# Logits copied ahead of the lower half of v, and a new order table, in a bucketed-attention and mixture-of-experts kernel

## The chip, the cores and the metric

The kernel runs on one core of a Trainium2 chip. Its time is the device time of one execution in microseconds (us); before the change it is 607.02 us, the median of three runs (606.85 to 607.43). The engines are TensorE (PE in the profile, its weight loads PEld), VectorE (DVE), ScalarE (ACT), GpSimd (POOL) and SyncE (SP), on whose queue nearly all DMAs are issued. Each engine takes its instructions in the order in which they were issued to it.

## The reference

Two layers follow each other, over 4 batches of 768 positions.

```python
# attention: 8 heads of 64; q and k are hashed to 6 sign bits each
q_bits = (q @ proj) > 0 ;  k_bits = (k @ proj) > 0        # 6 bits -> bucket
scores = where(q_bucket == k_bucket, (q @ k.T) / 8, -1e9)
x = softmax(scores) @ v                                   # heads side by side: 512 columns
# mixture of 4 experts, each a causal attention of width 64
logits = x @ w_gate                                       # 4 per position
topk = two largest logits;  w = softmax over these two
for e in range(4):
    qe, ke, ve = x @ wq[e], x @ wk[e], x @ wv[e]
    ye = softmax(causal(qe @ ke.T / 8)) @ ve @ wo[e]
    out += (e in topk) * w_e * ye
```

Everything is float32 in the reference. The kernel computes its products from pairs of float16 numbers, a high half and a low half.

## The kernel before, in words

**The units of work.** There are 32 units "L" (batch, head) of the first layer and 16 units "M" (batch, expert) of the second. `s_unit` (line 946) does one unit in chunks of up to 512 columns: two products into a PSUM tile `st`, two exponentials on ScalarE (`p` in float32, `ph` in float16), their difference `pl` on GpSimd, and three products per 128 columns into the PSUM tile `o`, with `ph` and `pl` against the high and low halves of v. `max_steps` (line 799) finds each row's largest score two units ahead: products into a PSUM tile `mx`, and VectorE's reductions of it into `pm`. A chunk of the lists `L_MAX`, `M_MAX` and `M_S` (lines 787 to 795) may have two parts; for these two products go into different columns of one tile, and each part is reduced by an instruction of its own. `shift_steps` (line 871) turns the maxima into a row: a product into `misc`, a copy to `row` on ScalarE or VectorE, and a DMA into the unit's `qa`, which the unit's `st` products read. `normalise` (line 1044) divides `o` by its sums; of the last unit it does a first half while products of the other half are still to come.

**The jobs beside them.** `prep_pair` and `proj_steps` make q and k, `xt_steps` transposes the first layer's result, `vproj_steps` (line 1118) makes v of the four experts and the gate's logits, `gate_steps` the gate's weights, `out_steps` and `last_out_steps` the output. `vproj_steps` has six tiles of 128 positions per batch, 24 in all: twelve products of 260 columns into a `misc` tile, then three readers of that tile: ScalarE writes the high half of v (`mvh`), VectorE the low half (`mvl`), and ScalarE or VectorE copies the 4 logits columns (`lg`).

**PSUM tiles.** Eight banks: three `st`, two `mx`, two `misc`, one `o`. Two engines' accesses to one tile are put in sequence in the order in which they are issued, whether or not they touch the same columns, readers among themselves too.

**The order.** The functions don't issue anything. They record 11,117 operations in a list (`Recorder.add`), some with two engines to choose from (`Recorder.copy`, line 128, offers ScalarE first and VectorE second). `Recorder.schedule` (line 163) then reads the table `ORDER` (line 216): compressed, four bytes for each operation. Two bytes say which of the operations still left is issued next, one which of its engines it takes, and one how many filler products (128 by 128 of ones, into the `o` tile) are issued ahead of it. So the table alone decides each engine's sequence, SP's and POOL's too, and the recorded list only gives the numbers that the table's places refer to.

```python
for take, alt, fill in zip((raw[0] + 256 * raw[1]).tolist(), raw[2].tolist(), raw[3].tolist()):
    order += [self.filler] * fill
    o = left.pop(take)
    order.append((o, o.alts[alt]))
```

All operations are issued by line 185, which is why every row of the profile has that line; rows are told apart by the tiles that they write and read.

Of the kernel before, what the change touches and what calls it, by code (L numbers as in the profile page):

```python
# [18 lines left out]
AX = mybir.AxisListType  # L19
# [96 lines left out]
class Recorder:  # L116
# [173 lines left out]
def tile_kernel(ctx, tc, q, k, v, proj, w_gate, wq, wk, wv, wo, out):  # L290
    nc = Recorder(tc.nc)
    B, HP, _, _, HS = q.shape
    _, KT, E, D = wq.shape
    Dm = KT * 128
    H, S = 2 * HP, 2 * HS
# [70 lines left out]
    for g in range(4):  # L366
        o = 32 * g
# [21 lines left out]
    for j in range(2):  # L389
        x = pbe[D * j:D * j + D, j]  # L390
# [143 lines left out]
    U = {}  # L534
# [538 lines left out]
    XT, G, XS = {}, {}, {}  # L1073
# [394 lines left out]
```

## Time and profile before

| | before |
|---|---|
| median of three runs | 607.02 us |
| the profiled execution's own time | 607.13 us |
| its span, first to last instruction | 605.3 us |
| TensorE busy, matmuls | 590.1 us |
| VectorE busy | 523.7 us |
| ScalarE busy | 516.7 us |
| GpSimd busy | 471.4 us |
| DMA, mean over the span | 85 GB/s |

The span is one profiled execution. A busy time counts an engine's instructions, not its waits; matmuls overlap one another and their ends are modelled, so that TensorE's busy time is no measure of how full the array is. A time in brackets behind a row is how long the engine sat idle before it, and the name behind the arrow is what ended that idle time.

### The profile page before, as it was taken

What the parts mean: (1) busy time and instruction counts of PE and PEld (TensorE: products, weight loads), DVE (VectorE), ACT (ScalarE), POOL (GpSimd) and SP (SyncE); (2) the same over time, 40 slices, a digit from 0 to 9 for tenths busy, and PEclk for the clock granted to TensorE, in tenths of its full rate; (3) what the DMA queues carried; (4) which work ended last, traced back from release to release, by engine and by line L of the source; (5) the groups of instructions that cost most, each with busy time, mean ns of one, the idle gap of its engine ahead of it and who ended that gap; (6) DMA issues with size and microseconds to landing.
All of it is one profiled execution on the core that took longest, in us unless ns stands there. A gap on an engine that the chain in (4) does not pass through costs nothing.

```text
span 605.3 us, 20342 instructions
## 1 busy us (share of the span) xinstructions
PE 590.1 (97%) x7754; PEld 432.6 (71%) x7754; DVE 523.7 (87%) x1440; ACT 516.7 (85%) x1132; POOL 471.4 (78%) x540
## 2 busy tenths in 40 slices
PE   7999999999999999999999999999999999999996
PEld 4788888778776777777667676777767677767663
DVE  6999999898899999888979999988988977557973
ACT  7989999999889899968969999997978978935774
POOL 8899989977687999858777889985866888942661
PEclk9999999999999999999999999999999999999999
DMA  6666353231512132341323143222222121001322
GB/s 189 170 191 191 86 139 78 53 101 52 147 46 57 40 91 61 85 122 26 98 81 95 38 117 102 60 86 76 69 88 82 46 48 36 17 21 35 89 72 106
DMA packets 36314, 51.23 MB, mean 85 GB/s; under 512 B 8212, under 2 KB 26104, under 8 KB 36216
## 3 DMA queue, kind: packets, MB, share of 16 engines
q1 hardware_dynamic: 36056, 49.93, 30.0%
q8 instruction: 61, 1.00, 0.7%
q14 instruction: 37, 0.30, 0.2%
q10 hardware_dynamic: 160, 0.00, 0.0%
HBM read 20.98 MB, written 6.29 MB: 45 GB/s over the span
## 4 chain that ended last, share of the span: by engine, by line
PE 78%; ACT 8%; DVE 8%; POOL 2%; issue 2%; DMA 2%; SPq 0%; DVEq 0%; ACTq 0%; POOLq 0%
PE misc L185 24%; PE st L185 24%; PE o L185 19%; PE mx L185 12%; ACT p L185 3%; ACT ph L185 2%; DVE pm L185 2%; POOL pl L185 1%; DVE pmw L185 1%; ACT xt L185 1%; DVE xt L185 1%; DMA qk<-M 1%; DVE qk L185 1%; DMA pbe<-in_proj_dram 0%; DVE scrap L185 0%
## 5 line engine op out<-in xcount | busy, mean ns | idle before, releaser
L185 POOL TENSOR_TENSOR pl<-p,ph 128x512 f16<-128x512 f32 x370 | 409.5, 1127 | 106.4 <-ACT p L185 31.2
L185 PE MATMUL st<-qk,qk 128*128 128x512 f16 (+12 forms) x928 | 229.8, 325 | 2.3 <-ACT p L185 1.2
L185 ACT ACTIVATE ph<-st 128x512 f16<-128x512 f32 x372 | 213.7, 609 | 13.3 <-PE st L185 9.2
L185 ACT ACTIVATE p<-st 128x512 f32<-128x512 f32 x372 | 215.5, 608 | 11.2 <-PE st L185 8.1
L185 PEld LDWEIGHTS <-ph 128*128 128x128 f16 x2880 | 168.2, 98 | 35.2 <-issue 5.8
L185 DVE TENSOR_REDUCE pm<-mx 128x2 f32<-128x512 f32 (+1 forms) x248 | 163.1, 674 | 10.6 <-PE mx L185 7.7
L185 PEld LDWEIGHTS <-pl 128*128 128x128 f16 x1440 | 133.3, 97 | 16.8 <-issue 4.2
L185 PEld LDWEIGHTS <-qk 128*128 128x128 f16 (+4 forms) x1248 | 109.1, 98 | 43.2 <-issue 6.8
L185 PE MATMUL o<-vh,ph 128*128 128x65 f16 (+1 forms) x1104 | 138.8, 194 | 0.3 <-DVE xp L185 0.3
L185 PE MATMUL o<-vh,pl 128*128 128x65 f16 (+1 forms) x1104 | 138.8, 193 | 0.3 <-POOL pl L185 0.3
L185 PE MATMUL o<-vl,ph 128*128 128x64 f16 x1104 | 138.2, 192 | 0.0
L185 PE MATMUL mx<-qk,qk 76*128 76x512 f16 (+2 forms) x464 | 134.3, 326 | 2.8 <-DVE pm L185 2.5
L185 PE MATMUL misc<-xt,wqk_h 128*128 128x384 f16 x256 | 58.6, 325 | 0.1
L185 DVE CUSTOM_DVE_ANT_0 scrap<-mx,causal 128x512 bf16<-128x512 f32 (+2 forms) x96 | 44.5, 463 | 8.0 <-PE mx L185 6.2
L185 DVE TENSOR_REDUCE pmw<-mx 128x2 f32<-128x512 f32 x68 | 44.9, 682 | 2.3 <-PE mx L185 2.0
L185 PE MATMUL o<-mvh,pl 128*128 128x65 f16 x336 | 40.6, 193 | 0.6 <-DVE yn L185 0.6
L185 PE MATMUL o<-mvl,ph 128*128 128x64 f16 x336 | 40.9, 192 | 0.0
L185 PE MATMUL o<-mvh,ph 128*128 128x65 f16 x336 | 40.6, 194 | 0.1
L185 POOL TENSOR_TENSOR vl<-vf,vh 128x384 f16<-128x384 f32 x32 | 29.5, 925 | 10.6 <-PE misc L185 5.1
L185 PEld LDWEIGHTS <-xt 128*128 128x128 f16 x324 | 29.5, 97 | 10.4 <-issue 1.2
L185 PEld LDWEIGHTS <-wqk_h 128*128 128x128 f16 x256 | 24.1, 97 | 13.9 <-issue 0.8
L185 PE MATMUL misc<-wvg_h,xt 128*128 128x260 f16 x192 | 32.1, 274 | 0.7 <-ACT row L185 0.7
(226 smaller groups left out, 1001.6 us busy)
## 6 DMA issues: line engine op xcount, KB each, us to landing
qk<-qk SPq DMA_DIRECT2D x128, 96.0 KB
natv<-in_v_dram SPq DMA_DIRECT2D x16, 384.0 KB
natq<-in_q_dram SPq DMA_DIRECT2D x15, 384.0 KB
natk<-in_k_dram SPq DMA_DIRECT2D x15, 384.0 KB
out_dram<-ot SPq DMA_DIRECT2D x20, 256.0 KB
qk<-qk SPq DMA_DIRECT2D x96, 48.0 KB
qk<-qk SPq DMA_DIRECT2D x8, 192.0 KB
qk<-M SPq DMA_DIRECT2D x48, 24.0 KB
```

The costliest lines, as they stand in the source:

```text
L185: getattr(getattr(self.nc, e), m)(*[real(x) for x in args], **{k: real(x) for k, x in kw.items()})
```

## The change

It has two parts. In `vproj_steps` the copy of the logits is recorded ahead of the low half of v:

```diff
             nc.scalar.activation(MVH[:, i, :, 0:D], pv, AF.Copy, scale=2.0 ** -16)
+            nc.copy(lg[:, i], p[:, E * D:W], XS[b][:, 2:3])
             nc.vector.scalar_tensor_tensor(MVL[:, i], pv, 2.0 ** -16, MVH[:, i, :, 0:D], op0=OP.mult, op1=OP.subtract)
-            nc.copy(lg[:, i], p[:, E * D:W], XS[b][:, 2:3])
             yield 864
```

And the table is another one; of its text only the beginning is shown:

```diff
 ORDER = (
-    "c-rlJX^bT2d0u^A-S^#9)z#Hqec#9QOwUZubkEGr%+9gPy}3M>BE4K*wnBljgy^6sSdb`LzLX$jC_r)|IdG6fN}@!8%mju5<X;5A2y6sF{v<G9|L_k(K%D%E6XpG?yLV=m%ZL=0<nFQ`"
...
+    "c-rlpX^b3adf)4<`|i5Bx~i+Y`o8a(>1%qrd+r&|3`vn39y*qi)+9wrkyc#El6E&<%ZTh`y^yiHh-Jg;>^d?wae%$xtdm{Ci2)-H5CaAh_=ADKK`tZ+VC;t=UMC2QAkSMpJu{>ztqw}0"
...
```

Decoded, both tables hold the same 11,117 operations, 7,609 of them products on TensorE. What differs:

- The sequence on every engine; the median product on TensorE stands 3 places from where it stood.
- Products into a PSUM tile and readers of that tile. In both tables 71 products stand behind a reader of the same tile (40 in `shift_steps`, 16 in `prep_v`, 15 into `o`). In the old table 19 more do: 11 into `mx`, 4 into `o` behind the first half of the last `normalise`, 1 into `st` behind the addition of the causal mask to the tile's other part, and 3 of the constants at the start. In the new table these 19 stand ahead of all readers of their tile.
- The readers of the 24 tiles of `vproj_steps`. The old table has 8 with `lg`, `mvh`, `mvl` in that sequence, 5 with `mvh`, `lg`, `mvl` and 11 with `mvh`, `mvl`, `lg`. The new table has `mvh`, `lg`, `mvl` in all.
- The engine of 85 operations: ScalarE has 1,152 instead of 1,149 of all operations, VectorE 1,341 instead of 1,344, GpSimd 536 as before. `lg` is copied by ScalarE 19 times instead of 13.
- The fillers, 87 instead of 75, all among the first 72 products; 26 instead of 8 stand ahead of the first product of the sign rows (`mx<-natq,pbe`).

## Rows read from the trace of the kernel before

**Rows 1.** The page: busy us of each engine, share of the span, instructions.

```profile
PE 590.1 (97%) x7754; PEld 432.6 (71%) x7754; DVE 523.7 (87%) x1440; ACT 516.7 (85%) x1132; POOL 471.4 (78%) x540
```

**Rows 2.** The page: the chain that ended last, share of the span by engine.

```profile
PE 78%; ACT 8%; DVE 8%; POOL 2%; issue 2%; DMA 2%; SPq 0%; DVEq 0%; ACTq 0%; POOLq 0%
```

**Rows 3.** Stretches: from:to, us, busy PE, PEld, DVE, ACT, POOL (instructions), PEclk, DMA share, GB/s.

```profile
180.00:210.00 30.00, 28.98 (x403) 20.60 (x400) 28.34 (x76) 28.23 (x62) 25.49 (x25) 1.00 0.20 49
...
360.00:390.00 30.00, 29.80 (x452) 21.90 (x450) 28.36 (x77) 29.02 (x65) 26.30 (x27) 1.00 0.35 95
```

**Rows 4.** Timeline at seven places of TensorE: start us, us, engine, line, operation [idle before <-releaser].

```profile
156.57 0.19 PE L185 MATMUL o<-vl,ph 128*128 128x64 f16 x1
156.86 0.55 DVE L185 TENSOR_REDUCE pm<-mx 128x1 f32<-128x384 f32 x1
157.46 0.22 PE L185 MATMUL mx<-qk,qk 65*128 65x128 f16 x1 [0.69 <-DVE pm L185]
...
180.09 0.34 PE L185 MATMUL o<-vs,fq 128*128 128x65 f16 x6
...
194.68 0.19 PE L185 MATMUL o<-vl,ph 128*128 128x64 f16 x1
195.64 0.22 PE L185 MATMUL mx<-qk,qk 65*128 65x128 f16 x1 [0.77 <-DVE pm L185]
...
370.95 0.19 PE L185 MATMUL o<-vh,ph 128*128 128x66 f16 x1
371.34 0.22 PE L185 MATMUL mx<-qk,qk 65*128 65x128 f16 x1 [0.20 <-DVE pm L185]
...
481.10 0.32 PE L185 MATMUL misc<-xt,wqk_l 128*128 128x384 f16 x1
481.87 0.22 PE L185 MATMUL mx<-qk,qk 65*128 65x128 f16 x1 [0.45 <-DVE pm L185]
...
544.15 0.19 PE L185 MATMUL o<-mvh,ph 128*128 128x65 f16 x1
544.50 0.27 PE L185 MATMUL mx<-qk,qk 65*128 65x256 f16 x1 [0.16 <-DVE pm L185]
...
586.44 0.38 PE L185 MATMUL st<-qk,qk 128*128 128x384 f16 x2
587.28 0.33 PE L185 MATMUL st<-qk,qk 128*128 128x128 f16 x2 [0.46 <-DVE st L185]
...
592.64 0.38 PE L185 MATMUL mx<-wo_h,xt 128*128 128x512 f16 x1
593.64 0.19 PE L185 MATMUL o<-mvh,pl 128*128 128x65 f16 x1 [0.62 <-DVE yn L185]
```

**Rows 5.** The logits' tile: copies on ACT (ns min/median/max); what ended idle time before (us, times).

```profile
L185 ACT ACTIVATE lg<-misc,xs x13: 239/263/265, 148.5 to 552.7; 128x4 f32<-128x4 f32 x13
...
  DVE mvl L185: 3.6, 6
```

**Rows 6.** Shift rows: a DMA in the chain, then the timeline of two units.

```profile
368.11 1.74 DMA qk<-row
...
179.93 0.27 ACT L185 ACTIVATE row<-misc 12x128 f16<-12x128 f32 x1 [0.61 <-DVE fr L185]
182.54 0.38 PE L185 MATMUL st<-qk,qk 78*128 78x512 f16 x1
...
461.96 0.25 ACT L185 ACTIVATE row<-misc 12x128 f16<-12x128 f32 x1
464.92 0.68 SPq L185 DMA_DIRECT2D qk<-row  x1
```

**Rows 7.** Timeline of the first 17 us.

```profile
3.66 1.49 PE L185 MATMUL mx<-natq,pbe 128*32 128x384 f32 x2
...
6.57 0.81 PE L185 MATMUL mx<-natq,pbe 128*32 128x384 f32 x2
...
14.32 1.80 ACT L185 ACTIVATE xt<-xt 64x384 fp32r<-64x384 f32 x3
```

More of the change, by code (lines that the diff above doesn't have):

```diff
@@ new lines @@
+    "mrf)TNw49Qh*GJ@6beEqUn=Gcc0T84eLwB{zN<QgLfp;eyl0>N+3bssldRrw-4aupa|(uh*(0K9;F0vztNBN+pL^=zaG3dvOemeUABme6A5s0s9=qiGmoHn%)P?9vvDk|*irTBM4uAjW"
+    "4cBp2&?a|dPq23!C;S;FWRHoJu({g)lKS`TvZ=iGTD4d~8Le{%G&a)>sjXJ)#1vKC0+u#6H`P-cEl~lA#kn>7tQd{<1oy^`8(~-PURB1*KMz@rW$ROi%(0I?nn=j5F&|4CX7bwG@X|{!"
+    "+4hS8@(WWcmHlwocl3y!xvuNZ^768-k4B@-&H0^&Eqz_z+;1A)#;DO4?d@s1ySwVnjuG@)8w?jKX9fe?uIc)4IIOg9$_q<NdZXJJ4$FqI2o(BtnZjc}LN-bzM=2D{Xx&Xzt5v(zQXMDa"
+    "gfGgLRZF{=;4ybdI7?*KZ8McJlgV&6pEo0x9Qul`n@0Z2c^y8EZ*1h4Y&l<=Ams|T(LRnVr=m_1NHmTSPu85vx**1j@vQ6lK5p1=l)Si~%BAATjFyhY`u)*J`xP(#Wf<<z_xnC37LUiP"
@@ new lines @@
+    "a%_U+P3Qxz2a{!4H`HV@DJBw$6NySC;#;g4HiJ<nCj6O1kVC_;@~ira4%45}v~)OZ7^bOt#sM1}ne6=OjFugb$9jsd)oN?~z7fsm^DO&NY{2dBKite_v+al|+P|Ij53ZajegFH(;y9P^"
+    "#cY6-Nja%osoh4ZTK&1~XGu7?+fAl(o|xg{4Y$=gbqYr5yK!%8tGxGEvE)YAw)AJ8&EtWbN~QP0yH13EYRjGwnTtd?`!=*NCVfOWra5z_-H63Zk2c)@=ZeNZV=6kM<3-G5*4O{$L}5L%"
+    "xtdp*>?r>>;7*&rnf#M{KAkS4;f-|m&J+q+&r4@A>8i@?Crf^!P)KdU4ERwuHeOo?(&<E;_Pu8oJ+J4{!Ftl3_o?Tr_3E?F!lG6#mBlZ7!8u1e0iW7?K1I{vBrOWlbvkN|zLGgYHzmXH"
+    "jfC#UbS)bNFQ9Xai=j|DgqI-HYSlTOtI*9VOojA}cZ>szE-^9j_JNO%fHe>Vr+0vpNEC}v$IZpEg8|G=wt7gc=2!mIEv-%XSI+8$=%RB%7`gfnI+5SiSKBKK%dz(QIx|}N7DP9;Ic0dj"
@@ new lines @@
+    "SH8lS;n!>J1rf)yU&IfOV$4U5s6ULMQFY6bu8hZ)HX8nDtc8?NK6J#A)e470p}_ErxgKFaBlUXs5Vbn-SaD%OZ5{|oySOtIRVzp9TmeSaDV5^xT(MB;M-z!?a0Z#ryVdwg;Mq%Cyca93"
+    "dFA7rnG&l<;&IO>Yum{!H&*tdnNz12$9GB5_3SK7+OZ^UvT?>R!aX=|VR`|lRx0fthuN^K;c$Bt4r^B5(#)}G47DW&79<kc59sXeojKF#pWZnYa+qBe*xEeKg#djuIG8yHoS>+OFq(8~"
+    "Jcbn;@2^6p__ied&M6t@ufH?crVg!O>xkiaj177{28%md87-^hu??YRd1Zb1#M&CQ##xcYMQUONJiih^YDPFrk|qvaPaLv)eoi}a_Uzf6t0y>pN(d}?dwV;Kn>uBm9h^}@2PSoLWLkqU"
+    "V;ZsbBTQp;wccGEcl&|)^p_49o3yg8o$EoWh^+Nj^^X4Ja=YK(SbB8f)2o`^xqMkW9~mwL$NumPepJ%0w%fhqJUnVGcF}x)*#BE<E?L{lW_Rv{c7jT$L!bYAQ7pe~C4LqNQ8@qk{>__l"
@@ new lines @@
+    "W%0S^p8MuEP46EZ;wi>&n6CG06Wll6xbnsuYw;<LllH)M1wlfH3Www2m<z$$bsv+3@D-i3tQ1m<#jdI%o0K8fD@s;QL3~LilGW<xs#Tdm*sXIp)M~A)z}jEC=3QlzG?`8&9)G-i86Xo&"
+    "Y@yI8fJvb90eF=b=3===A06$DnvXxe^vf5UOU?aXWL|r1<4j}y5_|64!7?z|t1oqGwezZaPKD(=`!i>cSXp}Lq4H_qvqvneqtft|i{WQ3JpJ^}jT<|~@YeR3#nTMKocioH0qz@XB>DBP"
+    "fBpLP>%We9;mtRLiFx4-V0r82&98m!%{QrkNd4AZxboSr(iHU@G~NF)K9=qeuU$pd&fe<)&oA&i|M~S-DDHo9-126N+y27(2KV{Tzy1ox{qob#zxbu&h$1HlMULke;UxY#&vUN;q9|W@"
+    "@xtZHH*elVtXo_7r!2>n*(s^r?*z{~so&mbiE|9g_Rhe|z1`hkQLkSQKlRj8;cF*$AgqMpT?1k@`}1t-Bo51xR4lgJCsS-P3G>cwY%D*5jadyqAkCsK7HD!~?wGpKw&73I^&}=Ym(1pL"
@@ new lines @@
+    "J<X76v{>@X4kg=4I1D<c(}~M+BGKa|>3j89Y;KNkRk{&~RiapGR!fajmC7W?IH?<x=aJ(K3DXgTu;;}+uhTIi5D*<}&Jv%udewTJFik>lUeXbt;Teugpaj9}=65nVcyT*pj+<sIqf%CR"
+    "QpRJFQwqpBJf;}@x!(i4_F}v3Eo}Z{wkKhrNvSDG%^p0|>vc&|D*wA6k)k}o7c-!S2I6|+bDnq$3pZ|*%c@eYa6+*NUL%Miw$q3kSzb=~5g{f7*lBn$jOWH<c-D2Te6{z-qF5Jfl?l|a"
+    "lE^BG6!YX;v85m5D}G&?u7aW<<yLI_i(d@>K?@Qu%Df~<^6rzSX>Ln2FYuQxfzx!iP-i0$DPehJ9fvm?3?u9_Vj}2Akc{m4d2()Ujs@>-S*1pUt{<?6aVJS3!NeH|l4!HI5ib@C%RPIP"
+    "9FK>i(U5L;LZBWk2$#oc^oK{B1ct-lLZKjtnNhl-I<*B=YiJttWK~&&K=CS8+NbctBHe7#B}Pglo~8X_achfC)6CDTtv&f9mj<!ur*LNG1{gj?9oa*=%*pE<Hu$2XP#%@ZMAJ$tr36--"
@@ new lines @@
+    "R9*Zi$W$yy)M+>>?ClmJScF95={TQ?C%}QKi3GhE6S#Pklm1Q=(2}(4hOWLutL3tNN!KkeCq$#BscV96Artgz$cV>Db)s}^BnO5LUMS`ueQFRcrHsB?+)3!kZ~x&RhQy5{z@c#HU-=6z"
+    "COiM=xGBKmtB@H3gI42lH40C^l$1e|Mm)xb158=wDq=_!!Pk^(^%<}yco!AGx-;~ly@Do;xr>XU=<;Bd^A1a{>1Lnfz!nf<WC)Atv?wRjaB8-km1RbV#l&=)=D6^ReKfI(%qj4ss+<C5"
+    "RxHAmA#!DL_~Icp9mFV_!O#-~us(WijbnG9o~9u)(BRGz&b>4Wk}q{E+Hn7lP!A{_;S`zqKeFT0arL{p$}rI|Pt)-@6{O8rJ=AV9V8_(_Jk_0}z5$dL7MjgP=|?SzDpYATTQQ2?{jOZd"
+    "SLzf+tyb;~wz~?;LQ(P>=g}<dB#1-3nadqUVnh(AW04go=mp_XS>b$56!qv?l9eJ6@n`{)x3I9l<3fh@eK!7UobHo(uq(Izy7o6U=4+8ksBD)?zF)8-aXacWM$Gqr9Q)gGCIm`Gwm~8l"
@@ new lines @@
+    "uNOgJCqp`v8!&gQ%Knv`^E@}ox>@&pMvmAM>pN=SI7Xph7%Z#Np;MtylH5t9GQ)ofD>B^JP}kS}AN*h~rmn0E`+aXk4PwiJ6+9tXCTfIuAaWHoC&iOW97iuj5#?89aV0ECsMq8EtDx$F"
+    "h6CR;Oy#dAl)&Y3d@8q*!}>xXMx(?q&a#PJc4tR-JMM@jTqo3I4uQqbLG)IX9JByUz*`ZAN!Ws52}evuL~+`IhlHdci@}0TZ61;<q)twx_7p*Yl7a?z0E1)^6&eoVb6o0Cuvil)dSMbO"
+    "FNC>$Dh-{WSdO7^Q$GBGLiW6DHg80;bjqDpn-KeGQv(^t4gQC~_4~?Tz|j{kPOiw>r%%^$q1e3@qEu>z!&?l?QE=7u>{^Loc!)iGwc4&$^I(Dt6&@n79B&qjH~>S!r5QH{h2Y|17Cy*k"
+    "Q}Y2XooY5GJ*iaaa+#un3Vvd%X)jFEE`5mTk<qB&PQU}Druz{buka4f6$*6xFuSn-;lIljHmD4w63_p8?XU2aheNPCt{)0@yCa_B7_TTXq7tbVi^}6-cQSuT5A0kge68YWmr%&%ovh<n"
@@ new lines @@
+    "md(ItxCF(~`j-ZS-X6u7n89FvzTaP6m70IOEJ-gt^UR1H)~Tlk13?gb!jT~hpg78xgp!lo7YI8ZPx7~5n$V-Epzm}h&k7hv;UTVAd`OO+;yh^=N~7&4nv^GN8yliH2u!6jwHezcBndjT"
+    "P;Qu}4CBgxktJ~@Z0zic>pGbC23&K9Rgw80MFURk$g-;4PFc=?`JF$XOqz)}s3HLul_65FtTkI`%r(HGCYjhU3&AXK8g#cf>Gc(!w|Ety5F{N&Ai!+po+wFejh1Dw@5vJJ0{BISPs7lY"
+    "w@n4l69mgjEUUAcMv0WlhG>dz4QRg6qxf$3(j|(5z&wSHP`Bx+TXt0blv8ysC=wLQOj0syOtwGfZiN+_VXMYwD;2Q43P(|?bgGtPg-rF0W-(JPR3~DhP^r@SQlVJP-?pVS(fAXXT#hV("
+    "UMQ6Y^?IgIW%3M@P3AM@a<Vw@q?{&mxNC6ofK-NMSN%ho?65Yycz|3eK!V%V^|?&1)xr}z$MdAB{u|YExb90Oe&vtqI4Dm?0_OU=oDhW3B1qVEx)6;nf3;G{9aPHSEtlgUeuiMpxv<A_"
@@ new lines @@
+    "?KUe$q3909L@!#7svhk)prM;h^JMs}ey|T^!>kw-4>=Q1I)zXiR2Z2uj6l5%6uqopighk@f?XQM^G=?WLXuP_OR^k~29^@IsvIOg67M=q7LO15NvdFNppt?GgM?&yy2mHU1ns!H4|5!$"
+    "v%O_KP`uHo3L=K6-~dGy{sm+&lQURaV?+7rP6nsq$m(#HAWPXYBpDzi$zKFm35zQ3<(FSBKzs#-CGpQC@Qx7g`-$g|TMe4pWQ^w#>p14nV%eV@t`7_C@Ijt$@hrz<*PAZ|9>`9Hg*bfF"
+    "A5RYEIEKS!udz~le6`JSOG^y5!Z1AnjD%&b)v65JWlk~;Y`lLT{+Ry+XIc2v>`{|<$o0*NtJNc{;;PN&kS;aAzwk!h=s4@}m(G_*in6YRm_AK+heMDV6Gcle-2yQf(2GnT%8veazt!w0"
+    ";D%kc(_!0zCDvJ<>%i!^iJ=w5=}y$tichivWJNZ;EeNF&%i`wu_xGoc%7yWSDvHV3df9@{)DZTZ9!Ei-_?=M5Yl0Qm;7?*~2aFSh!6X%Um00;!y#FkSg~H+fil5)u5U#UpYq6LAjE^#!"
@@ new lines @@
+    "X2u5tA9`#$mL0RjQmGXdEijpkuA50Ckp-!v|69Cm!b16D+bVpN&tsdi;&#%u6}P7>|HvPAz-~P+ZyDeF-a+!C^>$k{=b4a66bdzLXd!UO)K{~iq?U=Nv+QQ#u*RWex!>2du_bqVJz0KE"
+    "o@~~%)YI5ZcXwYGb}AJ~Vsa(4l)kk-6R}`lj+&w)>jnsL9AdL6vyl?vm6%dvdC%L9#}gYHUeXVR1O|&{g9%(j;^%J<=O8d7iuaIo0K!eEV5}hUd76VNd<Eppw^%gV+7ek7G9Ax{4}i=o"
+    "=(lkoC;4Nh*qS_j`qQkdM96p!va31z7Go~W(;&cUwcX~y>Z*|S%}6VNZvG}PSCW|qRj(_*_j?tZ25pzjedjyh5i?x<Hn`N&DgIZpRDu3#G@8sLlf`1PQaRA2(3$LESE3UeNuuKQIgpz!"
+    "&oEfkKL!bhr1c2Bk7d1#bE{TFzfa|V_(KTy5_TMxTa%x&uu`xDhUfeJ{-sO2?r4$QK=e=Om6a7l;caA`OcY6HY8rM5QDg#T*Jxxz7oaRDV`)d{;^?*-IXVHku7C|Q0tqq1hj<8n1@V-;"
@@ new lines @@
+    "c=Du-gH=4b`3HZnxw+I?5(WcToYbUFR9yNe5y5sA7CJ(hv%WEjRBGvs$v+O<E#cuReq}{~BJQuJnN{xwPtQ%ulxtj`gUNfM%Kd9maI-jcCArvPCM69Rl40ZU1Fld~K~aDu!Yid%WZ`rP"
+    ";=GUIQU6PUT|rSJm=VKqVDWLe6<kB$g3n6bE-$j#?4)zm8jDl%@ucrfo>)#C?~HG<`e(LSc4MQ(3Z^Ltx@k%+<BqUgnq;_${lD<OyjZvsc<=TclV%Js6*KBj?5~A)Vrsab)vCR|eyMnL"
+    "ONx<L#7o(9tCeY`@dfbVl`f0-VlU<E_48bg6LvD0CV&274L+v1(;&z^4{u0qjyNWEP~{~Tk}*goOfm@;c2prS8FYdY<#-(19N3ZEcX~4KN=F=xZk|vnD#&XvT@uA`1idHFJ3Bnj!1M;$"
+    "g&hfJV2XtOKZgpGg9?FVn>)_iFkmAL(`9g|&{{z|OqQmD`uzKGkAFi#9M^(aZ5}O59)d-Z7oe{_p;k*Q#0CG_HNRN&{mW2V{M>)J9LHXF(IX1{q?(@GO*)N|$3>ZS2Wrh4uEH4EP#7ie"
@@ new lines @@
+    "CQqJ>#df!LcD9l}4x?+rs?1EM1o|$_&5Lu`-LMb?#8#=Q7G<!=Jk(Pp5eF5)bCHO5IFFq2BOK`frO}kYK&o}{Jt<!*Nw?#-#RznBgVQ3Gy&NJ(C5yt1Xa>UsL6iwG8C)3VA=VP%R4N*U"
+    "=qRih%hQ-0q3Q5~#_}o)4}6z{Yz)_Bp*jkP$6;#I4z%GPPKq4nI78%Uo^6lE!UDH+`LZ;?6)vsTrY@@Tu16!vrvBT3W8*T?At<}8Q!MM=MoN~aQR)_bYuL>uWGrgXq#HDiw<WTf2F*}e"
+    "5aE>y7<r>mPZz4UlCRJ?d?;Nkt{0(ttW?U!w!_Nhdbvhdt86+w$E2FsO16A>X028|ckY$I?U>-cPO<oZBaxHGU}G!`g4biu9q1dXRKjD+Q|tWvFI*rY&79Rieuk=50cv)7lcm6_n$7VT"
+    "1jkadDY-7gKq!h9tVSd6{uZN7TFz>j%pB9w@+k(&&8%vgSkD#1VJIkZ0oMzM@jWT^%tik1X2QB{c({B(fv{C4;etiOpsdte3L}~gO;^=UCmIdG^m06C@x-A4rz|JI`gqI3&*v>7%UkVs"
@@ L287 @@
+    "eBuJi%<X4!bH<Dr@5!Ojy%JvNUNm~2tpNIfmqd4YQqbKTF}e$_&2rLAS<E_lzfBaHEyqVS5_G?Ia`tn`SzP`I%oNSc?GvBG(0wx(=o7mJ_p=G0nZv&K>mu}lyM#VD>yI8}3qudU^q`;e"
+    "4*G<x`V8Xk|92Dj+&9q7EN7;B7p{ih#V7BfJ2Qj)2=v-)j^5qud=ROK-sv#(p)Umb_?hJg>^}O?f8FtsPU}aWpWkV;=mB%=kE_F>kKeSSd(i0pw8M)YESEs{!|dD-zY;++W4ebUMDMk@"
+    "_=xTHeK+^ML)Tr1dGGoX=x$3DDR>OM%cF1qY5tvmm1q(ge!BC|n%?<`+#l#?j`-x+kNjuMm@#9<j2Sa#%$PA_#*7&=X3Ur|W5$dbGiJ<~F=NJz88c?gm@#9<j2Sa#+?oFm&mr{="
 )
```

86 lines of the change are left out of this document (17 added, 69 removed).

## The prediction

> **What bounds the kernel now.** I read four views, from the coarse to the fine. The page's table of engines comes first: TensorE is busy 97% of the span, VectorE 87%, ScalarE 85%, GpSimd 78% [rows 1]. The reader is to see that no second engine is at its limit over the whole span, and that TensorE leaves 605.3 - 590.1 = 15.2 us idle. The chain that ended last says the same: 78% of it is PE, and ACT and DVE have 8% each [rows 2]. So only two things shorten this kernel: less TensorE work, of which the change removes none, or fewer waits of TensorE. The table by stretches then tells where another engine could take over: DVE is at 28.3 and ACT at 28.2 of 30 us between 180 and 210, ACT at 29.0 between 360 and 390 [rows 3]; over the whole span they have 4 us idle in 30. Last comes the timeline of PE alone, where a wait is a late start with its releaser in brackets.
>
> **The waits that the change is about.** TensorE takes its products in order, so one that waits holds all behind it. At seven places a product into a PSUM tile stands, in the old table, behind a reader of another part of that same tile, and TensorE waits for that reader [rows 4]. The plainest: VectorE reduces the first, 384-column part of an `mx` tile from 156.86 to 157.41, and the second product into the same tile, 128 columns, starts at 157.46, 0.89 us after the product ahead of it. The granted clock is 1.00 of 2.4 GHz [rows 3], and at one column a cycle a 64- or 65-column product takes a slot of 0.03 us, one of 128 columns 0.05, of 384 0.16, of 512 0.21; six 65-column products in a row bear that out, 0.34 us with the last one's own 0.19, so 0.15 for five slots [rows 4]. Each wait is the distance of two starts less the slots between:
> - 157.46 - 156.57 - 0.03 = 0.86
> - 195.64 - 194.68 - 0.03 = 0.93
> - 371.34 - 370.95 - 0.03 = 0.36
> - 481.87 - 481.10 - 0.16 = 0.61
> - 544.50 - 544.15 - 0.03 = 0.32
> - 587.28 - 586.44 - 0.21 (two products, 0.16 and 0.05) = 0.63
> - 593.64 - 592.64 - 0.21 = 0.79
>
> Together 4.50 us. By the idle times in brackets, which count from a modelled end, it is 0.69 + 0.77 + 0.20 + 0.45 + 0.16 + 0.46 + 0.62 = 3.35 us.
>
> **Part 1, the products ahead of the readers.** Decoded, the old table has 19 products behind such a reader that the new table has ahead of it: 11 into `mx` (the second product of a two-part chunk of M_MAX), one into `st` (behind a mask addition), four into `o` (behind the first half of the last normalise) and three single-column ones of the constants. Twelve of the 19 cost no wait; the other seven are the 4.5 us. In the new table none is left, so these waits go: -4.5, or -3.35 by the brackets; I take the first, since starts are recorded and ends are modelled. What is late next: TensorE arrives up to 0.9 us sooner at its next tile, and the engine that frees it does not get the time. Two of the seven lie in the stretches where DVE or ACT has under 2 us in 30 to spare [rows 3]: 0.93 and 0.36 = 1.29 us that may come back at once as waits on `p`, `ph` or `pm`. Bounds 0 and 1.29; I take half, +0.65.
>
> **Part 2, the logits.** Each of the 24 tiles of `vproj_steps` has three readers. In the old table 11 tiles have the logits last, 8 first, 5 between; in the new one all 24 have them between `mvh` and `mvl`, 19 on ACT against 13. The three readers of one bank follow one another in any sequence, so the tile is held as long. ScalarE loses a wait: the logits waited for `mvl` six times, 3.6 us together [rows 5]. VectorE gains one: `mvl` begins one logits copy later in 11 tiles, 11 x 0.26 = 2.9 us if nothing else stands ready [rows 5]. Six copies more on ACT are 1.6 us of its 516.7. All this is off TensorE as long as the other `misc` buffer is free: bounds -3.6 and +2.9, taken as 0, since TensorE works on other tiles meanwhile and both engines have 4 us idle in 30. Without that cover it would be the 2.9.
>
> **Part 3, the rest of the table.** TensorE's 7,609 products are the same; their order is shifted by a few places nearly everywhere (half of them by no more than 3). 85 operations change between ACT and DVE or DVE and GpSimd, three net from DVE to ACT: under 2 us of work against some 80 us of idle time on either. Two places need a price.
>
> The shift rows: for 40 units a product into `misc`, a copy to `row`, a DMA and the unit's first `st` product follow each other. Counting TensorE's slots between the first and the last of these, the old table has at least 2.9 us and two units under 3.0; the new one at least 2.2 us and seven under 3.0 (2.23, 2.36, 2.46, 2.64, 2.65, 2.83, 2.92). The chain itself: 0.2 for a 128-column product [rows 4], 0.27 for the copy and 1.74 from issue to landing, 2.2 us [rows 6]; from above, a unit whose `st` product started 2.61 us after the copy's start without a wait gives 0.2 + 2.61 = 2.8 [rows 6]. By the first nothing waits, by the second 0.57 + 0.44 + 0.34 + 0.16 + 0.15 = 1.7 us. The landing of 1.74 is the measured one, so I take +0.2. `row`'s DMA stands on SP's queue, where nine places in ten hold another transfer than before; what is queued behind it there (`fq` rows, halves of the next units) is wanted later than the row itself.
>
> The first 17 us: 18 copies instead of 19 stand on ACT ahead of the row copy that starts the first `st` product, and ACT works through them without a gap (three take 1.80 us): a gain of up to 0.6 [rows 7]. 87 fillers of 128 columns stand on PE instead of 75; twelve more, at a slot of 0.05, cost up to 0.6 if they are in the way. Bounds -0.6 and +0.6, taken as 0: neither is nearer.
>
> The first signs product's two passes take 1.49 us at 3.66, the last one's 0.81 at 6.57, the same shape [rows 7]: the lower and then the upper of the array's two clock levels, 1.2 and 2.4 GHz. The Trainium skill, "TensorE: Matmul & The Clock Gate", Part 1, says that the array is throttled by default and that activity lifts the throttle. By it the 26 fillers that now stand ahead of that product (8 before) would have its passes at the upper level, and the sum would be 1.49 - 0.81 = 0.7 us lower. The rows tell against taking it: the passes' readers are four VectorE comparisons behind a VectorE queue that the new table makes longer by a copy, so the time would wait there. Leaving this paragraph out changes no number.
>
> **Sum.** -4.5 + 0.65 + 0 + 0.2 + 0 = -3.65 us. The profiled execution took 607.13 us, 605.3 of them the span and 1.8 around it, which the change doesn't touch; the median of the three runs, 607.02, is 0.1 lower. So 607.02 - 3.65 = 603.4 us, 0.6% faster. All far ends added: -4.5 - 3.6 - 0.6 = -8.7 at the best (598.3), and -3.35 + 1.29 + 2.9 + 1.7 + 0.6 = +3.1 at the worst (610.1). The ends lie 5.1 below and 6.8 above the sum; five separate costs hardly all go one way, so the forecast's own range is a third of that on each side: 601.7 to 605.6.
>
> **Rivals.**
> - The time comes back. For it: ACT and DVE are above 90% in several stretches and the chain changes engine often, so a TensorE that is early may just wait at `st` for `p`. Against it: only two of the seven waits, 1.29 us, lie in the two stretches of rows 3. If all but 0.5 us returns: 606.5, no change that can be told. Chance 0.20.
> - Slower, by shift rows held on SP's queue. SP issues in order and waits itself: a row copied at 461.96 to 462.21 was issued only at 464.92, 2.71 us late, and cost nothing because its unit had time [rows 6]. Were this to happen to the units that now have under 3.0 us, each would cost about 2.71 - 0.3 = 2.4 us. One such unit leaves a gain of 1.2, two (4.8) turn it to a loss of 1.2, three give 607.0 - 3.65 + 7.2 = 610.6; it decides from the second. Against it: what stands directly ahead of these seven in SP's new order are transfers of earlier units, whose sources are written long before. Chance 0.14, at about 610.
> - More than forecast. The other idle time of PE, 15.2 - 3.35 = some 12 us, lies at tiles that the new table moves too. If a quarter of it goes as well: 603.4 - 3 = 600.4. For it: from a chunk's `st` product to the first product that reads its `pl` the new table has 0.2 us more of TensorE's slots on average over 372 chunks; against: in 45% of them it has fewer. Chance 0.10.
>
> **How the numbers follow.** The forecast has the remaining 0.56. A measurement of this kernel can tell about 0.2%, 1.2 us, from no change. Faster than 605.8: 0.56 + 0.10 = 0.66; within: 0.20; slower than 608.2: 0.14. The range of 8 in 10 takes in the forecast's own 601.7 to 605.6, the returned time and the far edge of the larger gain: 600.4 to 608.0.
>
> **What would show it.** Right: in the new trace the second product of each two-part `mx` chunk starts one slot after the first or after products of other tiles, with no DVE `pm` in its brackets; PE's waits on DVE `pm`, `st` and `yn` fall from the 3.3 us of the seven to under 1; `mvl` waits for `lg`, and `lg` no longer for `mvl`. The return of the time would show as longer waits of PE on ACT `p` and `ph` after these places, a held row as a first `st` product of a unit released by DMA `qk<-row`. The prediction is wrong if the seven waits are gone and the span is not shorter by 1.2 us, or if any stay.

## The result, and the profile after

The new kernel takes 595.98 us (median of 4, 595.49 to 596.95), the old one beside it 606.93: ratio 0.982, 95% interval 0.9803 to 0.9837, 10.95 us less. The direction was forecast; the size, 3.65 us less, and the range, 600.4 to 608.0, were not. The profiled execution took 595.85 us, 594.1 of them the span.

The page of the new kernel, engines and chain, against [rows 1] and [rows 2]:

```profile
PE 584.8 (98%) x7766; PEld 434.3 (73%) x7766; DVE 521.1 (88%) x1437; ACT 514.7 (87%) x1135; POOL 469.9 (79%) x540
...
PE 85%; ACT 6%; DVE 5%; DMA 2%; issue 1%; SPq 0%; DVEq 0%
```

No engine does much less work: VectorE, ScalarE and GpSimd are each busy 1.5 to 2.6 us less than before. TensorE's idle time falls from 15.2 to 594.1 - 584.8 = 9.3 us. The other 5.3 us of the span stand in its busy time, though the products are the same: the modelled ends hide part of a wait. So below, waits are counted by starts.

TensorE's waits, first the old kernel's, then the new one's (waiter, who is waited for, us, times, longest; idle time of over 0.15 us alone, and by modelled ends):

```profile
PE mx L185 <- DVE pm L185: 2.5, 6, 0.8
PE misc L185 <- POOL one L185: 2.5, 1, 2.5
PE st L185 <- ACT p L185: 1.2, 3, 0.7
PE misc L185 <- ACT row L185: 0.7, 1, 0.7
PE o L185 <- DVE yn L185: 0.6, 1, 0.6
...
PE st L185 <- ACT ph L185: 0.5, 2, 0.3
PE st L185 <- DVE st L185: 0.5, 1, 0.5
PE o L185 <- DVE xp L185: 0.3, 1, 0.3
PE o L185 <- POOL pl L185: 0.3, 1, 0.3
...
PE mx L185 <- DMA qk<-M: 0.2, 1, 0.2
```

```profile
PE mx L185 <- DMA qk<-M: 2.4, 3, 0.9
PE o L185 <- DVE busy L185: 1.1, 1, 1.1
PE mx L185 <- DVE pmw L185: 0.3, 1, 0.3
PE st L185 <- DVE xt L185: 0.2, 1, 0.2
```

The reader is to see that not only `pm`, `st` and `yn`, the waits of the forecast, are gone from the list, but also `p`, `row`, `ph`, `xp` and `pl`, and that one kind is larger: `mx` waits for rows of M that a DMA copies into `qk`, 2.4 us against 0.2. (`one` and `busy` stand in the first microseconds.)

Counted by starts from 16 us on (the distance of two starts less the slot of the first, where over 0.07 us), TensorE lost 27.1 us in the old execution and 18.0 in the new one. The seven waits of the forecast [rows 4] went from 4.5 to 0, the rows of M in the new kernel are 1.09 + 0.77 + 1.04 = 2.9 us, and all the rest went from 22.6 to 15.1. So everything outside the seven waits, rows of M included, went from 22.6 to 18.0, a net -4.6, where the forecast had +0.2. The span fell by 11.2; of the 2.1 us that these 9.1 leave, some 1.9 are late starts of under 0.07 us each.

Where the time was gained shows when each product's start is compared with that of the same product in the old execution. The median lead of the new one, over the products of the 6 us from each time on (products change places, so it is good to about 1 us), is 0.6 us at 30, 0.1 at 60, 1.5 at 85, 2.2 at 140, 3.8 at 185, 4.9 at 200 and still 4.9 at 250, 6.9 at 265, 7.4 at 297, 8.0 at 375, 8.6 at 450, 9.2 at 530, 11.4 at 597. It comes in steps along the whole span.

The first of the seven places in the new kernel (timeline; x3 is three products in a row, the 384- and the 128-column part among them):

```profile
153.29 0.54 PE L185 MATMUL mx<-qk,qk 65*128 65x384 f16 x3
154.81 0.55 DVE L185 TENSOR_REDUCE pm<-mx 128x1 f32<-128x384 f32 x1
```

The reduction that TensorE waited for in the old kernel now comes behind the products. The stretches of [rows 3] in the new kernel show that the engines beside it got no freer; TensorE is simply never idle there:

```profile
180.00:210.00 30.00, 30.00 (x446) 22.03 (x444) 29.25 (x80) 29.11 (x66) 26.94 (x27) 1.00 0.24 62
360.00:390.00 30.00, 30.00 (x444) 22.19 (x443) 28.99 (x79) 29.16 (x69) 27.60 (x27) 1.00 0.34 92
```

The logits' tile, against [rows 5]: the copies `lg`, on whichever engine, no longer wait for `mvl` but only for `mvh` (second line), and now `mvl` waits for `lg` (third line, who waited for `lg`), as the forecast had it.

```profile
L185 ACT ACTIVATE lg<-misc,xs x19: 257/258/362, 146.1 to 550.1; 128x4 f32<-128x4 f32 x19
...
  ACT mvh L185: 3.6, 3
...
  DVE mvl L185: 5.9, 8
```

No unit's first `st` product is released by a DMA of `row` in this trace: the shift rows [rows 6] did not hold TensorE. (In three of the variants below that have the new order, a shift row of the first batch, named `roww`, held one by 0.2 to 0.3 us.)

### The profile page after: what moved, and what is told of

Its sections match the earlier page's. It is cut to its first block, busy times and chain, and to the rows that moved or that the text cites. A ratio compares the mean times of both kernels' runs of the same rounds, so it can differ in the third digit from the quotient of the medians.

```text
span 594.1 us, 20390 instructions
## 1 busy us (share of the span) xinstructions
PE 584.8 (98%) x7766; PEld 434.3 (73%) x7766; DVE 521.1 (88%) x1437; ACT 514.7 (87%) x1135; POOL 469.9 (79%) x540
## 4 chain that ended last, share of the span: by engine, by line
PE 85%; ACT 6%; DVE 5%; DMA 2%; issue 1%; SPq 0%; DVEq 0%
PE st L185 25%; PE misc L185 24%; PE o L185 21%; PE mx L185 13%; ACT p L185 2%; ACT ph L185 2%; DMA qk<-M 1%; DVE qk L185 1%; DVE xt L185 1%; ACT mx L185 1%; DMA qk<-qk 1%; DVE pm L185 1%; DVE pmw L185 0%; SPq L185 0%; ACT wst L185 0%
## 5 line engine op out<-in xcount | busy, mean ns | idle before, releaser
L185 ACT ACTIVATE p<-st 128x512 f32<-128x512 f32 x372 | 219.0, 621 | 18.0 <-PE st L185 12.4
L185 PE MATMUL st<-qk,qk 128*128 128x512 f16 (+12 forms) x928 | 226.5, 324 | 0.5
L185 ACT ACTIVATE ph<-st 128x512 f16<-128x512 f32 x372 | 216.6, 620 | 10.6 <-PE st L185 6.0
L185 PEld LDWEIGHTS <-ph 128*128 128x128 f16 x2880 | 165.1, 98 | 32.0 <-issue 4.4
L185 DVE TENSOR_REDUCE pm<-mx 128x2 f32<-128x512 f32 (+1 forms) x248 | 163.6, 674 | 11.3 <-PE mx L185 9.9
L185 PE MATMUL o<-vh,ph 128*128 128x65 f16 (+1 forms) x1104 | 136.3, 194 | 0.0
L185 PE MATMUL o<-vh,pl 128*128 128x65 f16 (+1 forms) x1104 | 135.7, 193 | 0.0
L185 PE MATMUL o<-vl,ph 128*128 128x64 f16 x1104 | 135.3, 192 | 0.0
L185 PE MATMUL mx<-qk,qk 76*128 76x512 f16 (+2 forms) x464 | 132.3, 325 | 2.5 <-DMA qk<-M 2.4
L185 PE MATMUL o<-mvl,ph 128*128 128x64 f16 x336 | 39.5, 192 | 0.0
```

Of the source, the lines that this page charges most:

```text
L185: getattr(getattr(self.nc, e), m)(*[real(x) for x in args], **{k: real(x) for k, x in kw.items()})
```

## Experiments: each part alone in the old table

All experiments change only the table, that is which operation is issued when and by which engine. The theory was that the gain is a sum of single waits, each made at one place of the order; the rivals, that the removed waits had caused the others (knock-on), that the logits carry the rest, or that the engine choices do. "Before" below is the old kernel run beside the experiment.

**Products ahead.** In issue order, at 16 places (the three of the constants stay):

```diff
  TensorE  mx[:, 0:384] <- qk, qk
+ TensorE  mx[:, 384:512] <- qk, qk
  VectorE  pm <- mx[:, 0:384]
- TensorE  mx[:, 384:512] <- qk, qk
```

> The old table with one edit: the 16 products of mx, st and o that stand behind a reader of their tile are issued ahead of that reader (the three of the constants stay), everything else in the old sequence. Waits add up (my forecast's step, and the theory now): the seven waits of TensorE go, 4.5 us less up to 0.65 that returns, so 602.4 to 603.4 us. Knock-on (rival: a wait of TensorE also delays ScalarE and GpSimd, which make TensorE wait again later): 7 us or more go, below 600. The time comes back: above 605.5. In the trace, by the first theory, the other waits of the old kernel (255.1, 276.4, 287.3, 292.5, 527.7 us) stay where they were, at their length.

604.14 us, ratio 0.9947 (0.9934 to 0.996): 3.2 us less. No knock-on: the other waits, at 255.1, 276.4, 287.3, 292.5 and 527.7, are all there at their length. All seven are gone; of the last two, 1.4 us, most (1.2 by starts) came back a little later (timeline):

```profile
590.37 0.36 DVE L185 TENSOR_TENSOR yn<-o,rden 128x192 f32<-128x192 f32 x1
590.78 0.19 PE L185 MATMUL o<-mvh,ph 128*128 128x65 f16 x1 [1.05 <-DVE yn L185]
```

**Logits between.** At the 19 tiles that had another sequence, `lg` put right behind `mvh`, on the new table's engine:

```diff
  ScalarE  mvh <- misc
+ ScalarE  lg <- misc
  VectorE  mvl <- misc, mvh
- VectorE  lg <- misc
```

> The old table with one edit: in all 24 tiles the logits copy stands between the high and the low half of v, on the engines of the new table (19 on ScalarE). My forecast: no difference, 606.9. The theory now: one of ScalarE's six waits for the low half, 1.11 us at 275.05, holds an exponential back, and TensorE waits 0.79 us for it at 276.45; that one goes, 605.9 to 606.4, and the five others cost nothing. Rival (the logits carry most of the gain that I did not forecast): 601 or less.

607.07 us, ratio 0.9995 (0.9986 to 1.0004): nothing that can be told, as forecast and against the theory's 605.9 to 606.4, but not because nothing happens. In the old kernel the copy that waited for `mvl` held an exponential back and TensorE with it:

```profile
275.05 0.26 ACT L185 ACTIVATE lg<-misc,xs 128x4 f32<-128x4 f32 x1 [1.11 <-DVE mvl L185]
275.21 0.59 ACT L185 ACTIVATE ph<-st 128x512 f16<-128x512 f32 x1
...
275.80 0.60 ACT L185 ACTIVATE p<-st 128x512 f32<-128x512 f32 x1
...
276.45 0.38 PE L185 MATMUL st<-qk,qk 78*128 78x256 f16 x2 [0.65 <-ACT p L185]
```

That wait (0.79 us by starts) is gone in the experiment, the 0.84 at 255.1 is down to 0.16, and others are new, the largest where `mvl` is now the last reader of a `misc` buffer (timeline of the experiment):

```profile
400.93 0.74 DVE L185 SCALAR_TENSOR_TENSOR mvl<-misc,mvh 128x256 f16<-128x256 f32 x2
...
401.40 0.35 PE L185 MATMUL misc<-qk,pbh 128*32 128x384 f16 x4 [0.86 <-DVE mvl L185]
```

**Both.**

> The old table with both edits, the 16 products ahead and the logits between. Waits add up: the sum of the two gains, 601.5 to 603. If the two parts named in the change are all there is to it, they give the whole gain: 596 to 597. Knock-on: 598 to 600.

604.12 us, ratio 0.9945 (0.9933 to 0.9958): the sum of the two. So what the change says of itself is worth 3.3 of the 10.95 us, and the forecast had that part nearly right (3.85). The other 7.7 us are in the rest of the table.

## Experiments: each part taken out of the new table

**Products behind again**, the first diff above the other way round. The products now come directly behind the reader (at three places the reader was moved ahead instead), not at the distance that they had in the old order:

> The new table with the 16 products put back behind the readers of their tile that stood ahead of them in the old one. Waits add up: about the 4.5 us return, 599.5 to 601 us. Knock-on: more than 7 us return, 603 or more. If the products were never the cause and the rest of the table is: under 1.5 us return, 597.5 or less.

605.84 us, ratio 0.9967 (0.9954 to 0.9979): some 9 us above the new kernel. By the number that is the rival's case (603 or more), but the trace, of an execution 3 us above the median, shows no knock-on: of 11.3 us more of late starts, 10.5 stand at the 16 products themselves. Twelve of them wait there, not seven, and eight of these waits are 0.6 to 1.9 us by starts, where the old ones were 0.3 to 0.9. Two things make them longer. At 8 of the 11 `mx` places less TensorE work lies between the first part's product and the second than in the old order (none instead of 0.75 us at the first), and at 8 of the 11 VectorE reaches the reduction later behind the first part's product (2.89 us instead of 0.37 at the fifth):

```profile
PE mx L185 <- DVE pm L185: 7.2, 8, 1.7
```

**Old sequence of the logits:**

> The new table with the three readers of the 24 tiles of v put back into the sequence and on the engines that the old table has. Waits add up: under 1 us slower than the new kernel, 596 to 597. Rival (the logits carry most of the gain that I did not forecast): 600 or more.

600.69 us, ratio 0.9889 (0.9875 to 0.9903): 4.2 us above the new kernel. By the number that is the rival's case too, but the same edit was worth nothing in the old order, so the logits don't carry the gain by themselves. `lg` as the last reader, behind other work of ScalarE, now holds `misc` buffers that TensorE wants at once, 2.2 us by starts at 404.10 and 548.86; the rest is smaller waits of several kinds:

```profile
PE misc L185 <- ACT lg L185: 1.9, 2, 1.5
```

**Old engines for the 85 operations** (in the table, the engine column alone), and the new engines in the old sequence:

> The new table's sequence with the engines of the old table for the 85 operations that changed theirs. Theory: the engines have idle time on either side, so within 1 us of the new kernel, 595.5 to 597. Rival (the new engine choices take work from whichever of ScalarE and VectorE is late, and carry the gain that I did not forecast): 599 or more.

> The old table's sequence with the new table's engines for the 85 operations. The new sequence with the old engines came to 609.5 us, 13 us above the new kernel. If the new choices are better by themselves: faster than the old kernel by some 5 us or more, 602 or less. Theory (a choice is good or bad only in its own sequence, since it decides which engine is late at one product): slower than the old kernel too, 609 to 620. My forecast (three operations net from VectorE to ScalarE, nothing to see): 606 to 608.

609.49 us, ratio 1.0033 (1.0022 to 1.0045), 13 us above the new kernel; and 631.32 us, ratio 1.0398 (1.0384 to 1.0412), 24 us above the old one. The first line is the page of the new sequence with the old engines:

```profile
PE 589.6 (97%) x7766; PEld 434.0 (71%) x7766; DVE 521.7 (86%) x1440; ACT 515.8 (85%) x1132; POOL 471.2 (78%) x540
```

VectorE's and ScalarE's busy times are those of the new kernel within 1.1 us; the balance says nothing, and 13 us are lost. Either set of choices is good only in the sequence that it came with. That a choice acts by deciding which engine is late at one product fits the waits; no experiment shows it for single choices. The three longest waits of the old sequence with the new engines, but for the start's:

```profile
PE mx L185 <- DVE pm L185: 5.4, 10, 1.2
PE misc L185 <- ACT row L185: 3.0, 4, 0.9
...
PE misc L185 <- DVE negh L185: 2.3, 2, 1.5
```

## Experiments: one table up to a seam, the other behind it

Sequence and engines of one table for the first 5,650 places, then what is left in the other's; and the new one for 250 to 297 us alone:

```diff
- for op in old: issue(op)
+ for op in old[:n]: issue(op)
+ for op in new: if op not yet issued: issue(op)
```

> The old table's sequence for the first half of the operations (to about 297 us) and the new one's for the rest. Theory (the gain is made of single waits, each gone at its place, and nothing is carried on): from 297 us on the new kernel gained 11.2 - 7.5 = 3.7 us, so 603.2 (602.5 to 604). Rival (the gain of one stretch rests on what the stretch ahead left behind, such as buffers free sooner): 605 or more.

> The new table's sequence for the first half of the operations (to about 288 us) and the old one's for the rest. Theory (single waits, each at its place): the first half's 7.5 us are kept, 599.4 (598.7 to 600.2). Rival (a sooner first half is lost again in a second half whose order is not made for it): 602 or more.

> The old table's sequence, but for the operations of the stretch from 250 to 297 us, which stand in the new table's sequence. In this stretch the old kernel has six waits of TensorE, 0.84, 0.37, 0.79, 0.47, 0.17 and 0.33 us (at 255.1, 259.0, 276.4, 287.3, 290.4 and 292.5), 3.0 us together, that the new one has not. Theory (single waits, gone by the order of the operations around them): 603.5 to 604.5. Rival (the gain of a stretch is only there with the new table ahead of it and behind it): 606 or more.

Old then new: 602.31 us, ratio 0.9919 (0.9906 to 0.9931), 4.9 us less. New then old: 602.23 us, ratio 0.992 (0.9902 to 0.9939), 4.9 less. Together 9.8 of the 10.95, so a stretch keeps most of its gain without the other. The first gained more than expected: of the two waits for rows of M that the new kernel has in its second half, the one of 0.77 us is not there. The second is by its time the rival's case (602 or more), but by starts its first half won 6.1 us, in the new kernel 5.8. It lost at the seam: 2.4 us by starts at 300.33, at an `mx` product that reads rows of M. The profile names no releaser; the last copy of these rows was issued only at 298.29:

```profile
298.29 0.62 SPq L185 DMA_DIRECT2D qk<-M  x1
...
300.33 0.38 PE L185 MATMUL mx<-qk,qk 76*128 76x512 f16 x1 [2.21 <-issue]
```

The window: 605.24 us, ratio 0.9971 (0.9962 to 0.998), 1.8 us less, between the two expectations. All six waits are gone, 3.0 us, and two are new at the seams (0.3 us at 252.0, 0.8 at 297.4). So in this stretch the gain is single waits, and the seams cost some of it.

## Experiments: repairs of the new kernel

TensorE's three longest waits in the new kernel are all for rows of M. SP's queue ahead of the first (timeline):

```profile
220.57 1.44 SPq L185 DMA_DIRECT2D qk<-qk  x1
222.11 0.62 SPq L185 DMA_DIRECT2D qk<-M  x1
222.78 0.58 SPq L185 DMA_DIRECT2D qk<-qk  x1
223.46 0.61 SPq L185 DMA_DIRECT2D qk<-M  x1
...
225.65 0.38 PE L185 MATMUL mx<-qk,qk 76*128 76x512 f16 x1 [0.92 <-DMA qk<-M]
```

An issue takes SP some 0.6 us; M was written by 220.7, and the second copy went out at 223.46, behind a transfer that had been ready since 219.6. The other two waits are at 336.19 and 476.26.

```diff
  SP       ...
+ SP       natv <- v            (prefetch; was issued at 219.90, now some 8 us sooner)
  SP       qk <- M              (222.11)
+ SP       qk <- M              (was 223.46)
  SP       qk <- qk             (222.78)
- SP       qk <- M
...
+ SP       qk <- qk             (was 470.61; holds back the rows of M at 474.35)
  SP       out <- ot            (468.14)
...
+ TensorE  ten products of st, o and misc
  TensorE  mx <- qk, qk         (336.19)
```

> The new table with three repairs, at the three places where TensorE waits longest in the new kernel, all for rows of M copied by DMA (1.09 us at 225.65, 0.77 at 336.19, 1.04 at 476.26): a load of natv moved ahead on the queue and one copy of M's rows ahead of another transfer; a copy of a half of q and k ahead of an output; ten products issued ahead of the one that waits. Theory (each wait is a matter of one place): up to 2.9 us faster than the new kernel, 593 to 594.5. Rival (the time comes back at the next products): 595.5 or more.

594.71 us, ratio 0.9794 (0.978 to 0.9807), between the two expectations. Two repairs hold (1.07 us at 225.65 and 1.05 at 476.26 by starts), the third gives a new wait of 0.58 us at 339.24 for `pm`. And this trace is 1.5 us behind the new kernel's from the first 30 us on. So four kernels together:

```diff
# new_queue_only: the two repairs on SP, without the ten products; new_queue_head also:
- TensorE  misc <- pat          (two products, 4.17, wait for GpSimd's pat)
  TensorE  mx <- natq, pbe      (first signs product)
+ TensorE  misc <- pat          (the two)
```

> The new kernel unchanged, beside its variants on the same chip: 595.5 to 597 us. Its first products on the sign rows of k take 1.48 or 2.77 us for four, by whether the array has reached its upper speed before them, so its times should scatter by some 1.5 us, more than the old kernel's 0.7.

> The new table with two repairs on SP's queue alone (natv's load and one copy of M's rows at 210 to 224 us, a half of q and k ahead of an output at 468 us), without the ten moved products. Theory (single waits): 1.09 + 1.04 = 2.1 us faster than the new kernel beside it, ratio to it 0.9965. Rival (repairs come back elsewhere): under 1 us faster.

> The same two repairs, and the two products of a constant that wait for GpSimd at 4.2 us put behind the first product on the sign rows. Theory (a wait of 0.3 us there lets the following products run at the lower speed, 1.3 us more): on average 0.3 to 1 us faster than the queue repairs alone, and less scatter. Rival (the first product on the sign rows waits for its load anyway): no difference.

> The old table to 16 us (its fillers too), the new one for the rest. In the two traces the new kernel is 0.7 us ahead at 16 us and keeps it. Theory: 0.7 us slower than the new kernel beside it. Rival (the new head is the faster one only in some executions): no difference, and less scatter.

New kernel again 596.67 us, ratio 0.9813 (0.9799 to 0.9828); queue repairs 595.46, 0.9794 (0.9779 to 0.9809); queue repairs and head 593.13, 0.9768 (0.9755 to 0.978); old head 595.08, 0.9819 (0.979 to 0.9847). The queue repairs' interval overlaps the new kernel's, so by times alone they are not shown; by starts against the first trace of the new kernel they win 1.08 and 1.06 us at their places. (In the second trace of the unchanged kernel the three waits are 1.17, 0.98 and 0.60 us: the same places, not the same lengths.) With the head the kernel is faster than the new one beyond both intervals, by some 3 us; the queue repairs' interval meets its own at the edge (0.9779 and 0.978), so the head's share, 1.6 us by the ratios and more than the 0.3 to 1 expected, is less sure. Its five runs lie within 1.3 us (592.79 to 594.08; the new kernel's 594.48 to 597.23). It is the fastest of all.

The head (timeline), in the new kernel's two traces and in the last repair:

```profile
4.30 1.49 PE L185 MATMUL mx<-natq,pbe 128*32 128x384 f32 x2
...
5.99 1.48 PE L185 MATMUL st<-natk,pbe 128*32 128x384 f32 x4
7.30 0.81 PE L185 MATMUL mx<-natq,pbe 128*32 128x384 f32 x2
```

```profile
4.58 0.20 PE L185 MATMUL misc<-one,pat 1*32 1x1 bf16 x2 [0.35 <-POOL pat L185]
4.72 1.49 PE L185 MATMUL mx<-natq,pbe 128*32 128x384 f32 x2
...
6.42 2.63 PE L185 MATMUL st<-natk,pbe 128*32 128x384 f32 x4
```

```profile
4.17 1.49 PE L185 MATMUL mx<-natq,pbe 128*32 128x384 f32 x2
...
5.92 2.00 PE L185 MATMUL st<-natk,pbe 128*32 128x384 f32 x4
```

Where TensorE had stood idle for 0.35 us ahead of the signs products, the four on `natk` took 2.63 us, and without it 1.48 or 2.00. In two variants with this head, though, they took 1.48 us behind 0.23 and 0.26 us of idle time there (the old sequence of the logits, the old engines). In the old kernel they took 1.79 and in variants with its head 1.77 to 2.77, without such idle time, but there a later product waits for GpSimd's `pbd` until 8.5 us in most of them and hides it. So the idle time goes with the slow passes in the new head; that it causes them is not shown. The old head before the new rest was not slower by 0.7 us: no difference, the rival's case, though with more scatter (593.73 to 600.3), not less. So the 0.7 us that the new kernel's trace shows at the head is one execution's luck, not part of the gain.

## Why the prediction was wrong

- **What bounds the kernel**: right. TensorE's products stayed the same; its waits fell.
- **Part 1**: right in mechanism, near in size: -3.85 forecast, -3.2 (-4.0 to -2.4) measured alone. The 0.65 us of return was taken at the two places where VectorE or ScalarE is full; 1.3 returned, 1.2 of it at the tail.
- **Part 2**: 0 forecast, 0.3 less measured, which can't be told from 0. The reason given, that TensorE works on other tiles meanwhile, was wrong at single places: 1.6 us of waits go and nearly as much comes.
- **Part 3, the failing step.** "The rest of the table" was put at +0.2, by pricing only two places where the new order is tighter. By starts everything outside the seven waits went from 22.6 to 18.0 us, -4.6: -7.5 at other places, +2.9 at the rows of M. By times the rest of the table is worth 7.7 us; the 1.9 us of late starts under 0.07 us, and the 1.2 that return at the tail in the old order and not in the new one, are about the difference. That is the case named "more than forecast"; its size, a quarter of the idle time and 3 us, and its chance, 0.10, were too small, and its mechanism was half of it. Its evidence was an average of TensorE's slots over 372 chunks, and an average can't see single waits. Looking at each wait does. TensorE starts late by about what the reader of a buffer needs, from the start of the last product that it reads to its own end, less the TensorE work that stands in between. At some places the new order puts more work there: 1.26 us became 2.07 at the product that started 0.33 us late at 359.75, 1.68 became 3.56 at 292.54, 0.91 became 1.91 at 434.72, 1.07 became 1.80 at 215.22. At four of the larger waits it does not (255.11, 276.45, 527.72 and 180.67, 0.4 to 0.8 us each): there the work is the same within 0.25 us, and the reader is done 0.6 to 1.2 us sooner, since its engine takes its work in another order.
- **The shift rows** cost nothing, as forecast, and the rival built on them did not happen. Its mechanism did, with another transfer: two of the three waits for rows of M, 2.1 of the 2.9 us, are copies issued late on SP. The third, at 336.19, is not: its copy was issued 0.7 us after M was written and took 3.5 us.
- **The head**: 0 forecast, and on average about that. The 26 fillers ahead of the first signs product started 0.107 us apart, not the 0.05 of the forecast's slot, and did not change its two passes in this trace, 1.49 us as before (the variant with the old engines had 0.83). By the rule of the Trainium skill weighed in the prediction ("TensorE: Matmul & The Clock Gate", Part 1) they could have run at the upper level; this trace does not agree with that use of it, and leaving it out of the sum was right.
- **The engines** of the 85 operations were priced by their sum, under 2 us. Exchanged, they cost 13 and 24 us.

The largest of these four waits, old and new (timelines; without a bracket there was no idle time of over 0.15 us):

```profile
252.77 0.22 PE L185 MATMUL misc<-identh,negh 128*72 128x128 f16 x1
...
254.80 0.27 ACT L185 ACTIVATE row<-misc 12x128 f16<-12x128 f32 x1
...
255.11 0.49 PE L185 MATMUL misc<-wvg_h,xt 128*128 128x260 f16 x3 [0.68 <-ACT row L185]
```

```profile
246.88 0.22 PE L185 MATMUL misc<-identh,negh 128*72 128x128 f16 x1
...
247.73 0.27 ACT L185 ACTIVATE fr<-misc 12x128 f16<-12x128 f32 x1
...
248.09 0.72 PE L185 MATMUL misc<-wvg_h,xt 128*128 128x260 f16 x5
```

The last of ScalarE's two copies ends 2.3 us behind the product in the old order and 1.1 in the new one.

What stays open: the parts don't add up to one account. In the old order Part 1 is worth 3.2 us, in the new one its absence costs 9, in part because the edit there leaves less TensorE work between the two parts than the old order had. The 7.5 us are shown as waits that are gone; they are not divided between sequence and engine choices, since an order with TensorE's sequence from one table and the other engines' from the other can't be carried out (it has cycles).

## What to carry to other kernels

When an order is replaced as a whole, list every wait of the bound engine, and for each look whether the new order puts more work between the releaser and the waiter or lets the releaser run sooner; the named edits may be the smaller part. Judge an engine choice or an edit within its sequence: busy times that agree within 1 us went with 13 us of difference, and an edit worth nothing in one order was worth 4 us in another. A trace whose waits have a common cause, here rows behind other transfers on one queue, says where the next few microseconds are.

## What the runs showed of the hardware

- The same four products on `natk` took 1.48 to 2.77 us while the granted clock's column reads 1.00 for every half microsecond of that stretch. Their starts are 0.32 us apart where they are fast (the new kernel's first trace) and 0.64 where they are slow (its second), a factor of two, as between 2.4 and 1.2 GHz. So in the first microseconds only the durations tell at which of its two levels the array runs.
- Rows of M of 24 KB, issued at 332.73, released their product at 336.19, 3.5 us later; at 223.46 it took 2.2 and at 474.35 1.9. In the second trace of the same kernel the three took 3.7, 2.2 and 1.9, so the place decides more than the execution; why the first takes longer is not shown. The Trainium skill, "DMA: Bandwidth & Descriptors", "Latency and other measured facts", has a fixed cost of about 2 us, most of it the latency of HBM and smaller when HBM is less loaded. The 1.9 to 2.2 agree with its size, though these copies go from SBUF to SBUF; the 3.5 and 3.7 are more.
